# The way from attention to MLP in a fused kernel: weight memory laid out anew, rows of g spread by transfers, a rewritten tail

## The chip, the core and the metric

The kernel runs as one program on one core of a Trainium2 chip. The metric is the device time of an execution in microseconds (us). The engines are TensorE (PE, with its weight loads as PEld), VectorE (DVE), ScalarE (ACT), GpSimd (POOL) and SyncE (SP), whose queue issues the kernel's transfers. Each engine works through its instructions in the order of the program.

## The reference

Three blocks follow one another, all in float32:

```
attention (B 4, H 8, S 576, D 64; 2304 tokens of 512 after the heads are joined)
    q, k rotated by cos/sin;  attn = softmax(q k^T / 8);  x = attn v
soft MoE (8 experts, 4 slots each, so 32 slots; F 1024)
    logits = x @ phi                       # phi [512, 32]
    d = softmax over tokens (axis 0);  slot_input = d^T @ x
    slot_out[e] = relu(slot_input[e] @ w1[e]) @ w2[e]
    c = softmax over slots (axis 1);   x = c @ slot_out
MLP (512 -> 2048 -> 512)
    h = x @ w_in;  g = h * sigmoid(h);  out = g @ w_out
```

## The kernel before

**Attention.** Sixteen pairs of heads are worked through in one stream in which an order of PE is written out by hand, with tables of steps (W_LOADS, W_OUT_AT, BATCH) that say at which step of a pair a further task is put in. The MoE weights come as 64 loads of 512 KB, w_0 to w_63: w1 is w_0 to w_31, for layer 1, and w2 is w_32 to w_63, for layer 2. The first 23 (NWA) have memory of their own, the next four lie in two tiles of the rotary stage, and all further ones in the pool `wb`, which is opened after the attention in memory that the attention's pools leave. A load into such memory waits for the last instruction that used what lay there. SP issues all loads in the order of their numbers, and a load that waits keeps the next ones back; eight transfers at most are under way, since there are eight semaphores for them. Chunks of w_out whose numbers stand in W_OUT_EARLY are loaded and converted during the attention.

**The tail of the attention.** The soft MoE's sums over tokens are kept over half-batches. For the last one (`h1` in the code) PE makes logits `lgh1`, ACT and DVE the exponentials, PE the transposed weights `dps5`, DVE copies them to `dh1`, PE multiplies them with the tiles x12 to x15 (`sps5`), and `slots` merges the sum into `s_b0`, transposes it to `si` (the slot inputs) and works out the denominator `den`. `lt` gets the last transposed logits.

**The MoE layers.** Layer 1 (line 871) multiplies `si` with w1, in two halves of four experts; layer 2 (line 892) the hidden rows with w2, each expert in a column group of 32. Between the quarters of layer 2 other tasks are put: transposes of the combine weights `c` to `cs` (`t0`, `t1`, `t3`). `slot_t` copies layer 2's sum to `o`, transposes it, and copies it to `so`, the slot outputs.

**The MLP.** Since x = c @ slot_out, the kernel multiplies slot_out with w_in once, which gives 32 rows of g for each block of columns, spread over partitions and split in a high and a low part (`gs0`, `gs1`); `hps` = gs × cs is then the hidden layer. The first 128 columns come from `g0_ps`, the next 384 from `g_product(0)` and `g_all`, and three further blocks of 512 from `g_product(1)` to `(3)`, each followed by 16 copies that spread its rows (`g_copy`, line 1103 on ACT and 1105 on DVE). The main loop has 3 blocks of tokens × 16 chunks of 128 hidden columns. A step has one chunk's sigmoid, split and 6 × 3 products with w_out (`ops`, lines 1154 to 1156); G_STEPS says behind which product of the first steps a g product or its copies stand. A chunk of w_out is 512 KB of 64-bit words which `narrow` converts (ACT `hw`, two DVE operations), and `split_hl` splits into `wo_hi` and `wo_lo`. Chunks 0 and 1 are converted together as `wf_first`, ahead of the loop.

## Time and profile before

| | us |
|---|---|
| median of 3 runs | 571.57 (571.24 to 571.92) |
| the profiled execution's own time | 573.27 |
| its span on the core | 571.5 |
| PE busy | 540.4 |
| DVE busy | 316.9 |
| ACT busy | 307.9 |

The span is the time from the first to the last instruction of the profiled execution. Busy times overlap between engines; the granted clock of PE was 0.982 of full speed as a mean over the span. Of the stages, the attention ends at about 300.6 us, layer 1 at 317, layer 2 at 338, and the main loop starts at 346.

### The profile page before, as it was taken

How to read it: one execution, taken by the hardware profiler on the slowest of the kernel's cores; microseconds unless marked ns; L12 is line 12 of the kernel's file. 1: busy time of each engine (PE TensorE's matmuls, PEld its weight loads, DVE VectorE, ACT ScalarE, POOL GpSimd, SP SyncE). 2: the span in 40 equal slices, each digit the busy share in tenths (PEclk: the TensorE clock that was granted, in tenths of full speed). 3: DMA queues.
4: the chain of work that ended last, by engine and by line, in shares of the span. 5: the costliest groups of instructions: out<-in, count | busy, mean ns of one | idle time of the engine just before them, and what ended most of it. 6: DMA issues, size and time to landing. Idle time of an engine off the chain costs nothing.

```text
span 571.5 us, 15141 instructions
## 1 busy us (share of the span) xinstructions
PE 540.4 (95%) x6219; PEld 438.1 (77%) x6219; DVE 316.9 (55%) x841; ACT 307.9 (54%) x612; POOL 111.3 (19%) x96
## 2 busy tenths in 40 slices
PE   5599999999999999999979989899999999999997
PEld 2378989898897998888853337677888888888885
DVE  4756666766666567654130457697454444544442
ACT  2366667666767566664421327987554433544332
POOL 4933332313333323200000021133000000000000
PEclk9679999999999999999998999999999999999999
DMA  8226777635665575743799895422020000200003
GB/s 301 95 56 206 266 244 278 203 116 172 224 231 172 207 265 166 249 166 107 296 322 382 306 359 179 135 93 75 0 93 18 1 1 1 96 16 0 2 0 111
DMA packets 36773, 88.70 MB, mean 155 GB/s; under 512 B 10560, under 2 KB 11872, under 8 KB 34784
## 3 DMA queue, kind: packets, MB, share of 16 engines
q1 hardware_dynamic: 36694, 87.73, 44.3%
q8 instruction: 49, 0.80, 0.6%
q14 instruction: 20, 0.16, 0.1%
q10 hardware_dynamic: 10, 0.00, 0.0%
HBM read 78.20 MB, written 7.60 MB: 150 GB/s over the span
## 4 chain that ended last, share of the span: by engine, by line
PE 76%; ACT 10%; DVE 5%; DMA 4%; issue 3%; POOL 1%; SPq 1%; ACTq 0%; DVEq 0%
PE u L386 10%; PE ops L1156 10%; PE ops L1154 10%; PE ops L1155 10%; PE st L353 8%; PE psmx L300 3%; PE st_r L366 3%; PE l L871 3%; PE hps L1049 3%; ACT e L357 3%; PE xps L414 3%; DMA w_out_raw<-in_w_out_dram 2%; PE psmx L316 2%; ACT relu L308 2%; PE u L380 2%
## 5 line engine op out<-in xcount | busy, mean ns | idle before, releaser
L1056 DVE TENSOR_TENSOR hps<-hps,g 128x384 f32<-128x384 f32 x96 | 49.8, 561 | 84.6 <-ACT g L1053 84.3
L1053 ACT ACTIVATE g<-hps 128x384 f32<-128x384 f32 x96 | 42.3, 490 | 82.3 <-PE hps L1049 81.9
L1154 PE MATMUL ops<-wo_hi,ghi 128*128 128x512 f32 x216 | 84.7, 392 | 0.0
L1155 PE MATMUL ops<-wo_lo,ghi 128*128 128x512 f32 x216 | 84.4, 391 | 0.0
L1156 PE MATMUL ops<-wo_hi,glo 128*128 128x512 f32 x216 | 84.3, 390 | 0.0
L321 DVE CUSTOM_DVE_ANT_0 relu<-psmx,relu 128x288 f32<-128x288 f32 x140 | 57.7, 455 | 47.1 <-ACT e L357 36.3
L357 ACT ACTIVATE e<-st 128x512 f32<-128x512 f32 (+1 forms) x128 | 76.4, 650 | 10.9 <-PE st L353 10.9
L386 PE MATMUL u<-v,e 128*64 128x65 f32 x2048 | 80.6, 225 | 0.0
L386 PEld LDWEIGHTS u<-v,e 128*64 128x64 f32 x2048 | 71.5, 139 | 6.2 <-issue 3.0
L308 ACT ACTIVATE relu<-psmx 128x576 f32<-128x576 f32 x62 | 40.1, 652 | 51.7 <-PE psmx L300 33.6
L259 POOL TENSOR_TENSOR raw<-raw,tab 128x576 f32<-128x576 f32 x29 | 41.8, 1442 | 132.8 <-DMA raw<-in_qk_dram 96.7
L1062 DVE TENSOR_TENSOR glo<-hps,ghi 128x384 fp32r<-128x384 f32 x96 | 49.4, 552 | 5.0 <-ACT ghi L1059 1.8
L1059 ACT ACTIVATE ghi<-hps 128x384 fp32r<-128x384 f32 x96 | 45.6, 494 | 10.2 <-DVE hps L1056 10.1
L1156 PEld LDWEIGHTS ops<-wo_hi,glo 128*128 128x128 f32 x216 | 40.6, 188 | 8.5
L1155 PEld LDWEIGHTS ops<-wo_lo,ghi 128*128 128x128 f32 x216 | 40.6, 188 | 7.5 <-issue 0.4
L1154 PEld LDWEIGHTS ops<-wo_hi,ghi 128*128 128x128 f32 x216 | 40.6, 188 | 7.5 <-issue 0.2
L256 POOL TENSOR_TENSOR raw<-raw,tab 128x576 f32<-128x576 f32 x29 | 42.0, 1447 | 0.0
L353 PE MATMUL st<-hi 64*128 64x256 f32 (+1 forms) x256 | 39.7, 302 | 0.0
L353 PE MATMUL st<-mq,neg_a 64*128 64x256 f32 (+1 forms) x256 | 39.1, 297 | 0.6 <-DMA mq<-m 0.6
L353 PE MATMUL st<-hi,lo 64*128 64x256 f32 (+1 forms) x256 | 38.9, 296 | 0.0
L353 PE MATMUL st<-lo,hi 64*128 64x256 f32 (+1 forms) x256 | 38.9, 296 | 0.0
L397 DVE TENSOR_SCALAR r<-u 128x4 f32<-128x4 f32 (+1 forms) x32 | 5.2, 164 | 49.7 <-PE u L388 30.1
(223 smaller groups left out, 998.7 us busy)
## 6 DMA issues: line engine op xcount, KB each, us to landing
w<-in_w_dram SPq DMA_DIRECT2D x64, 512.0 KB
raw<-in_qk_dram SPq DMA_DIRECT2D x14, 1152.0 KB
w_out_raw<-in_w_out_dram SPq DMA_DIRECT2D x16, 512.0 KB
w_in_raw<-in_w_in_dram SPq DMA_DIRECT2D x12, 512.0 KB
v<-in_v_dram SPq DMA_DIRECT2D x16, 325.0 KB
out_dram<-os SPq DMA_DIRECT2D x18, 256.0 KB
raw<-in_qk_dram SPq DMA_DIRECT2D x4, 576.0 KB
w_in<-w_in SPq DMA_DIRECT2D x8, 256.0 KB
```

The source lines that it names most:

```text
L308: act.activation(out=r, in_=pair[:, :, 0:HS], func=ACTF.Relu)
L321: dve.tensor_tensor_reduce(out=r[:, hd], in0=t[hd], in1=r[:, hd], scale=1.0, scalar=-3.0e38, op0=ALU.add, op1=ALU.max, accum_out=mxs[p % 2 ...
L353: pe.matmul(st[:, hd, 0:n], lhsT=a, rhs=b, start=i == 0, stop=i == 3, skip_group_check=True)
L357: act.activation(out=e[:, :, 0:n], in_=st[:, :, 0:n], func=ACTF.Exp, scale=0.125)
L386: pe.matmul(u[q:q + 64, 2 * i + hd], lhsT=e[:, hd, o:o + 64], rhs=x[:, hd], start=n == 0 and i + hd == 0, stop=n == 4, skip_group_check=True)
L1053: act.activation(out=g[i], in_=t[i], func=ACTF.Sigmoid)
L1056: dve.tensor_tensor(out=t[i], in0=t[i], in1=g[i], op=ALU.mult)
L1059: act.activation(out=ghi[:, i], in_=t[i], func=ACTF.Copy)
L1062: dve.tensor_tensor(out=glo[:, i], in0=t[i], in1=ghi[:, i].bitcast(F32), op=ALU.subtract)
L1154: pe.matmul(t, lhsT=a, rhs=wo_hi[k], start=k == 0, stop=False)
L1155: pe.matmul(t, lhsT=a, rhs=wo_lo[k], start=False, stop=False)
L1156: pe.matmul(t, lhsT=b, rhs=wo_hi[k], start=False, stop=k == 15)
```

## The change

- FREED gives the 20 weights of the pool `wb` other places: the order of the loads stays, but the sixth and seventh (w_33, w_34) get the pool's positions 16 and 17, and later ones the positions that they had. The attention's own pools are laid out in another order beneath.
- The memory of the rotary table (`tab`) becomes a pool of its own that stays open: w_27 is loaded into it, and later the split chunk 11 of w_out lies there.
- The tail: `xps15_1` and the other transposes stand elsewhere, `slots` no longer scales and adds on DVE but multiplies `s_b0` with a scaled identity `ss` and adds the second sum in PSUM, `si` is one copy, `den` comes behind (`total`), and ACT copies `lt`.
- `slot_t` copies `o` in two halves, on ACT and DVE. Chunk 0 of w_out is loaded early in place of chunk 12, so that only chunk 1 is left in `wf_first`, and it is converted behind the first products. Products of the first two token groups stand ahead of `g_all`.
- `g_copy` becomes 16 transfers on SP for each g product, in place of 12 copies on ACT and 4 on DVE, right behind the product.
- In the attention another of the two tiles for `relu` is used at u = 4.

```diff
-W_LOADS = (14, 18, 24, 27, 34, 37, 45, 54, 64, 66, 76, 86, 96, 102, 108, 114, 127, 129, 125, 135, 133, 123, 137, 145, 148, 134, 139)
+W_LOADS = (14, 18, 24, 27, 34, 37, 45, 54, 64, 66, 76, 86, 96, 102, 108, 114, 127, 129, 125, 135, 133, 123, 137, 145, 148, 134, 139, 138)
 SCALES = -19
-W_OUT_EARLY = (3, 6, 9, 12)
+W_OUT_EARLY = (0, 3, 6, 10)
 W_OUT_AT = (23, 43, 83, 113)
 EARLY = -10
+WO_TAB = 11
+FREED = (0, 1, 2, 3, 4, 16, 17, 5, 6, 7, 8, 9, 10, 11, 12, 18, 19, 13, 14, 15)
 WO_SLOT = {12: 13, 13: 14, 14: 15, 15: 16}
 QO = (0, 256, 576)
 QN = (256, 320)
 
-G_STEPS = (5, 7, 16, 19, 28, 14, 23, 37, 46, 53, 58)
-ACT_QUADRANTS = (0, 1, 2)
+G_STEPS = (5, 22, 52)
+LOAD_STEP = 28
+CONV_STEPS = (14, 23, 37, 44)
...
+    p_tab = ctx.enter_context(tc.tile_pool(name="tab", bufs=1, side=left))
...
+        elif n == 4:
+            w_sb[i, h, e] = p_tab.tile([128, 2, S], F32, tag="tab", name=f"w_{m}").rearrange("p t s -> p (t s)")[:, 0:1024].rearrange("p (k f) -> p k f", k=k)
...
-            p_tab, p_k, p_relu, p_14, p_soft, p_q, p_15, p_e, p_v, p_s, p_r = (mkpool(n, 1) for n in ("tab", "k", "relu", "p14", "soft", "q", "p15", "e", "v", "s", "r"))
+            p_k, p_relu, p_14, p_q, p_15, p_e, p_v = (mkpool(n, 1) for n in ("k", "relu", "p14", "q", "p15", "e", "v"))
+            xqp = mkpool("xq", 6)
+            p_s, p_soft = mkpool("s", 1), mkpool("soft", 1)
             xp = mkpool("xp", 4)
-            xqp = mkpool("xq", 6)
+            p_r = mkpool("r", 1)
...
-                r = p_e.tile([128, 2, QN[1]], F32, tag=f"e{u}", name=f"relu{p}_{u}")[:, :, 0:HS] if p == 0 and u in (2, 3) else relus[u % 2]
+                r = p_e.tile([128, 2, QN[1]], F32, tag=f"e{u}", name=f"relu{p}_{u}")[:, :, 0:HS] if p == 0 and u in (2, 3) else relus[1 if u == 4 and p > 1 else u % 2]
...
-                        act.activation(out=s_b[0][64:128], in_=s_b[0][64:128], func=ACTF.Copy, scale=sc[64:128, 5:6])
+                        ps["ss"] = p_r.tile([128, 3, NSLOT], F32, tag="dh0", name="ss")[:, 0]
+                        dve.tensor_scalar(out=ps["ss"], in0=stack_i[:, 0:NSLOT], scalar1=sc[:, 5:6], scalar2=None, op0=ALU.mult)
...
-                def slots():
-                    acc = s_b[0]
-                    for j in range(2):
-                        w = slice(256 * j, 256 * j + 256)
-                        dve.scalar_tensor_tensor(out=acc[0:64, w], in0=acc[0:64, w], scalar=sc[0:64, 5:6], in1=ps["s"][0:64, w], op0=ALU.mult, op1=ALU.add)
-                    t2 = ps_mx.tile([128, 2, 512], F32, tag="mx", name="si_ps")
-                    for j in range(2):
-                        t = t2[:, j]
-                        for k in range(2):
-                            c0 = 256 * j + 128 * k
-                            pe.matmul(t[:, NSLOT * k:NSLOT * k + NSLOT], lhsT=acc[:, c0:c0 + 128], rhs=stack_i[:, 0:NSLOT], start=True, stop=True)
-                        dve.tensor_copy(out=si[:, 2 * j:2 * j + 2], in_=t[:, 0:64].rearrange("p (k s) -> p k s", k=2))
+                def slots(t):
+                    o = hb[1][0:64, 0:DM]
+                    act.activation(out=o[:, 0:256], in_=ps["s"][0:64, 0:256], func=ACTF.Copy)
+                    dve.tensor_copy(out=o[:, 256:512], in_=ps["s"][0:64, 256:512])
+                    for k in range(4):
+                        pe.matmul(t[:, NSLOT * k:NSLOT * k + NSLOT], lhsT=s_b[0][:, 128 * k:128 * k + 128], rhs=ps["ss"], start=k == 0, stop=False, skip_group_check=True)
+                    for k in range(4):
+                        pe.matmul(t[:, NSLOT * k:NSLOT * k + NSLOT], lhsT=o[:, 128 * k:128 * k + 128], rhs=stack_i[0:64, 0:NSLOT], start=False, stop=True, skip_group_check=True)
+                    dve.tensor_copy(out=si, in_=t[:, 0:4 * NSLOT].rearrange("p (k s) -> p k s", k=4))
+
+                def total():
                     dve.tensor_tensor(out=scs[:, 3:5], in0=sc[:, 3:5], in1=sb[:, 3:5], op=ALU.mult)
...
-            for i in range(NWA + 4):
+            for i in range(NWA + 5):
...
-            h1[0]((0, 1, 2))
+            h1[0]((0,))
+            x_15(1)
+            h1[0]((1, 2))
             assert not tasks, tasks
             h0[3]()
             h0[5]()
-            x_15(1)
             h1[0]((3,))
             h1[2]()
             h0[4]()
             h1[3]()
+            h0[6]()
+            h0[8]()
+            h1[5]()
             h1[4]()
-            h0[6]()
-            h1[5]()
-            h0[8]()
+            t = ps_mx.tile([128, 2, 512], F32, tag="mx", name="lt3_ps")
             h1[6]()
-            t = ps_st.tile([128, 2, 512], F32, tag="st", name="lt3_ps")[:, 0]
+            h1[7](t[:, 1])
             for i, (o, n) in enumerate(CHUNKS[3]):
-                pe.transpose(t[0:n, NSLOT * i:NSLOT * i + NSLOT], hb[2][0:32, o:o + n], ident[0:32, 0:32])
-            h1[7]()
-            dve.tensor_copy(out=lt[:, 15:19], in_=t[:, 0:4 * NSLOT].rearrange("p (c s) -> p c s", c=4))
-            dve.tensor_copy(out=lt[0:64, 19], in_=t[0:64, 4 * NSLOT:5 * NSLOT])
+                pe.transpose(t[0:n, 0, NSLOT * i:NSLOT * i + NSLOT], hb[2][0:32, o:o + n], ident[0:32, 0:32])
+            act.activation(out=lt[:, 15:19], in_=t[:, 0, 0:4 * NSLOT].rearrange("p (c s) -> p c s", c=4), func=ACTF.Copy)
+            act.activation(out=lt[0:64, 19], in_=t[0:64, 0, 4 * NSLOT:5 * NSLOT], func=ACTF.Copy)
+            h1[9]()
...
-        for i in range(NWA + 4, NW):
-            slot_w(i)
-        for i in range(NWA + 4, NW):
+        for i in range(NW - NWA - 5):
+            slot_w(NWA + 5 + FREED.index(i))
+        for i in range(NWA + 5, NW):
...
-            act.activation(out=o, in_=op[g], func=ACTF.Copy)
+            act.activation(out=o[:, 0:256], in_=op[g][:, 0:256], func=ACTF.Copy)
+            dve.tensor_copy(out=o[:, 256:512], in_=op[g][:, 256:512])
...
-        load_wo(0)
...
-            t, h = (wa.tile([128, 2, 512], F32, tag=f"w{i}", name=n) for i, n in ((3, "wf_first"), (4, "hw_first")))
-            for k in range(2):
-                first.append((t[:, k], narrow(raw_w.pop(k), t[:, k], None, None, hw=h[:, k])))
+            t, h = (wa.tile([128, 512], F32, tag=f"w{i}", name=n) for i, n in ((3, "wf_first"), (4, "hw_first")))
+            first.append((t, narrow(raw_w.pop(1), t, None, None, hw=h)))
 
         first = []
         layer2(1, (t0, t1, t3))
         slot_t(1)
 
-        for f in first[0][1]:
-            f()
...
+        elif k == WO_TAB:
+            t = p_tab.tile([128, 2, S], F32R, tag="tab", name=f"wo_hl{k}")
+            wo_hi[k], wo_lo[k] = t[:, 0, 0:DM], t[:, 1, 0:DM]
...
-    def g_copy(n, r):
-        for q in range(4):
-            c0 = 512 * (n % 2) + 128 * r
-            o, i = gs2[n // 2][32 * q:32 * q + 32, c0:c0 + 128], gfull[n][q // 2][32 * r:32 * r + 32].bitcast(F32)
-            if q in ACT_QUADRANTS:
-                act.activation(out=o, in_=i, func=ACTF.Copy)
-            else:
-                dve.tensor_copy(out=o, in_=i)
+    def g_copy(n):
+        for r in range(4):
+            for q in range(4):
+                c0 = 512 * (n % 2) + 128 * r
+                sp.dma_start(out=gs2[n // 2][32 * q:32 * q + 32, c0:c0 + 128].bitcast(F32), in_=gfull[n][q // 2][32 * r:32 * r + 32].bitcast(F32))
...
+    def products(j, k, i, ghi, glo):
+        if k == 0:
+            ops[j, i] = ps_o.tile([128, DM], F32, tag="o", name=f"ops{j}_{i}")
+        t = ops[j, i]
+        a, b = ghi[:, 128 * i:128 * i + 128], glo[:, 128 * i:128 * i + 128]
+        pe.matmul(t, lhsT=a, rhs=wo_hi[k], start=k == 0, stop=False)
+        pe.matmul(t, lhsT=a, rhs=wo_lo[k], start=False, stop=False)
+        pe.matmul(t, lhsT=b, rhs=wo_hi[k], start=False, stop=k == 15)
...
-        (wf0, _), (wf1, n1) = first
+        wf1, n1 = first[0]
+        split_hl(0, wf_early[0], dve)
...
-        hidden(*seq[0], between=lambda: (split_hl(0, wf0, dve), g_product(0)))
+        hidden(*seq[0], between=lambda: g_product(0))
         n1[0]()
+        for i in range(2):
+            products(0, 0, i, *gt[0, 0])
...
-    for x, f in zip(G_STEPS, (lambda: g_product(1), lambda: copies(1), lambda: g_product(2), lambda: copies(2), lambda: load_last(1),
-                              lambda: conv_last(0), lambda: conv_last(1), lambda: conv_last(2), lambda: conv_last(3), lambda: g_product(3), lambda: copies(3))):
-        extra.setdefault(divmod(x, 6), []).append(f)
-    ops = {}
+
+    def put(x, f):
+        extra.setdefault(divmod(x, NI), []).append(f)
+
+    for n in range(1, 4):
+        put(G_STEPS[n - 1], lambda n=n: g_product(n))
+        put(G_STEPS[n - 1], lambda n=n: g_copy(n))
+    put(LOAD_STEP, lambda: load_last(1))
+    for k, x in enumerate(CONV_STEPS):
+        put(x, lambda k=k: conv_last(k))
```

In SP's queue, the loads around the first one that waits for the attention's last matmuls stand so before (w_39 to w_46; the names of the semaphores that a load waits for are in brackets, DMAHW being the one of the transfer eight places ahead):

```order
L120 DMA w_39_4990<-in_w2_dram 128x2x512 [waits DMAHW5_49]
L120 DMA w_40_4991<-in_w2_dram 128x2x512 [waits DMAHW6_49]
L120 DMA w_41_4992<-in_w2_dram 128x2x512 [waits DMAHW7_49]
L120 DMA w_42_4993<-in_w2_dram 128x2x512 [waits DMAHW0_49]
L120 DMA w_43_4994<-in_w2_dram 128x2x512 [waits DMAHW1_49,DVE_49,PE_49]
L120 DMA w_44_4995<-in_w2_dram 128x2x512 [waits DMAHW2_49,Activation_49]
L120 DMA w_45_4996<-in_w2_dram 128x2x512 [waits DMAHW3_49]
L120 DMA w_46_4997<-in_w2_dram 128x2x512 [waits DMAHW4_49]
```

and so in the change (w_31 to w_38):

```order
L126 DMA w_31_4985<-in_w1_dram 128x1024 [waits DMAHW5_49]
L126 DMA w_32_4986<-in_w2_dram 128x2x512 [waits DMAHW6_49,PE_49]
L126 DMA w_33_4998<-in_w2_dram 128x2x512 [waits DMAHW7_49,DVE_49,PE_49]
L126 DMA w_34_4999<-in_w2_dram 128x2x512 [waits DMAHW0_49]
L126 DMA w_35_4987<-in_w2_dram 128x2x512 [waits DMAHW1_49]
L126 DMA w_36_4988<-in_w2_dram 128x2x512 [waits DMAHW2_49]
L126 DMA w_37_4989<-in_w2_dram 128x2x512 [waits DMAHW3_49]
L126 DMA w_38_4990<-in_w2_dram 128x2x512 [waits DMAHW4_49,Activation_49]
```

The wait for DVE and PE together stands at w_43 before, and at w_33 in the change; the numbers of the loads go on in order in both.

On PE, at the end of the attention, the rows from the last `sps5` matmuls to the first of layer 1 are these before (`lt3_ps` are the transposes for `lt`, `si_ps` those for `si`):

```order
L565 MATMUL sps5_4918<-x12_3946,dh1_4862 32x64 x2
L565 MATMUL sps5_4918<-x13_4242,dh1_4862 32x64 x2
L565 MATMUL sps5_4918<-x14_4541,dh1_4862 32x64 x2
L565 MATMUL sps5_4918<-x15_4751,dh1_4862 32x64 x2
L842 MATMUL lt3_ps_4935<-cst_sb_73,last_logits_4826 128x32 x4
L842 MATMUL lt3_ps_4935<-cst_sb_73,last_logits_4826 64x32
L580 MATMUL si_ps_4943<-cst_sb_73,s_b0_77 128x32 x4
L871 MATMUL l1_0_0_5037<-w_0_653,si_79 32x512
L871 MATMUL l1_0_0_5037<-w_1_777,si_79 32x512
```

and these in the change:

```order
L574 MATMUL sps5_4922<-x12_3946,dh1_4864 32x64 x2
L574 MATMUL sps5_4922<-x13_4242,dh1_4864 32x64 x2
L574 MATMUL sps5_4922<-x14_4543,dh1_4864 32x64 x2
L574 MATMUL sps5_4922<-x15_4753,dh1_4864 32x64 x2
L584 MATMUL lt3_ps_4921<-ss_4902,s_b0_80 128x32 x4
L586 MATMUL lt3_ps_4921<-cst_sb_76,last_logits_4828 128x32 x4
L852 MATMUL lt3_ps_4921<-cst_sb_76,last_logits_4828 128x32 x4
L852 MATMUL lt3_ps_4921<-cst_sb_76,last_logits_4828 64x32
L881 MATMUL l1_0_0_5039<-w_0_653,si_82 32x512
L881 MATMUL l1_0_0_5039<-w_1_777,si_82 32x512
```

The transposes for `si` are now twice four, the second from a copy of the sum, and stand ahead of those for `lt`.

In the main loop, the copies that spread the rows of `g_product(1)` stand on ACT before, between the split of step 2 and the sigmoid of step 3:

```order
L1059 ACTIVATE ghi0_2_5491<-hps0_2_1_5500 128x384
L1095 ACTIVATE gh1_5536<-g_ps1_5519 128x128
L1103 ACTIVATE gs0_5343<-gh1_5536 32x128 x2
L1103 ACTIVATE gs0_5343<-gl1_5537 32x128
L1103 ACTIVATE gs0_5343<-gh1_5536 32x128 x2
L1103 ACTIVATE gs0_5343<-gl1_5537 32x128
L1103 ACTIVATE gs0_5343<-gh1_5536 32x128 x2
L1103 ACTIVATE gs0_5343<-gl1_5537 32x128
L1103 ACTIVATE gs0_5343<-gh1_5536 32x128 x2
L1103 ACTIVATE gs0_5343<-gl1_5537 32x128
L1053 ACTIVATE g0_3_0_5573<-hps0_3_0_5571 128x384
L1053 ACTIVATE g0_3_1_5580<-hps0_3_1_5578 128x384
```

In the change ACT has no such rows, and SP's queue has the transfers there, `x2` for two of them:

```order
L130 DMA w_out_raw5_5488<-in_w_out_dram 128x1024
L130 DMA w_out_raw9_5742<-in_w_out_dram 128x1024
L1112 DMA gs0_5342<-gh1_5535 32x128 x2
L1112 DMA gs0_5342<-gl1_5536 32x128 x2
L1112 DMA gs0_5342<-gh1_5535 32x128 x2
L1112 DMA gs0_5342<-gl1_5536 32x128 x2
L1112 DMA gs0_5342<-gh1_5535 32x128 x2
L1112 DMA gs0_5342<-gl1_5536 32x128 x2
L1112 DMA gs0_5342<-gh1_5535 32x128 x2
L1112 DMA gs0_5342<-gl1_5536 32x128 x2
L130 DMA w_out_raw7_5616<-in_w_out_dram 128x1024
L130 DMA w_out_raw8_5661<-in_w_out_dram 128x1024
```

The loads of w_out chunks 7 and 8 stand behind the sixteen transfers.

## Rows read from the trace of the kernel before

**Rows 1.** The page: busy time, share of the span and instructions of PE.

```profile
PE 540.4 (95%) x6219; PEld 438.1 (77%) x6219; DVE 316.9 (55%) x841; ACT 307.9 (54%) x612; POOL 111.3 (19%) x96
```

**Rows 2.** Busy time of each engine by stage, granted clock, DMA share, GB/s.

```profile
283.00:300.60 17.60, 13.55 (x235) 9.86 (x232) 6.14 (x24) 4.92 (x14) 0.00 (x0) 1.00 0.90 316
300.60:317.20 16.60, 16.60 (x136) 5.98 (x137) 2.93 (x5) 2.73 (x5) 2.23 (x2) 0.90 0.91 335
317.20:338.10 20.90, 20.47 (x166) 7.97 (x161) 8.90 (x24) 5.07 (x12) 0.00 (x0) 1.00 0.99 372
338.10:346.05 7.95, 5.07 (x83) 3.75 (x83) 4.63 (x8) 5.55 (x13) 4.37 (x3) 1.00 0.43 174
346.05:375.00 28.95, 27.11 (x173) 20.83 (x172) 22.34 (x50) 24.48 (x62) 3.86 (x3) 1.00 0.48 164
```

**Rows 3.** PE's waits from 283 to 375: in total, times, longest.

```profile
PE hps L1049 <- DVE glo L1062: 1.8, 3, 1.2
PE l L871 <- DVE lt L845: 1.6, 1, 1.6
PE hps L1049 <- DVE gs L929: 1.0, 1, 1.0
...
PE g_all L1110 <- ACT gf L1092: 0.7, 1, 0.7
...
PE lgh L514 <- ACT xt L418: 0.5, 1, 0.5
```

**Rows 4.** Waits of SP's own queue from 255 to 350, columns as in rows 3.

```profile
SPq L120 <- PE l L871: 14.4, 4, 7.6
...
SPq L120 <- PE st L353: 10.5, 2, 10.2
```

**Rows 5.** Busy time by stage, columns as in rows 2, around a stop of SP.

```profile
268.00:280.00 12.00, 11.42 (x229) 10.26 (x227) 2.91 (x8) 5.76 (x10) 0.00 (x0) 1.00 0.91 345
280.00:286.00 6.00, 5.69 (x124) 5.08 (x120) 0.76 (x3) 2.53 (x5) 0.00 (x0) 1.00 0.45 155
286.00:298.80 12.80, 10.64 (x171) 7.28 (x167) 4.88 (x16) 3.80 (x11) 0.00 (x0) 1.00 0.90 318
```

**Rows 6.** SP in order of time from 296.84: start, length, issue.

```profile
296.85 2.71 SPq L120 DMA_DIRECT2D w<-in_w_dram  x5
```

**Rows 7.** The chain that ended last, 283 to 302: start, length, what.

```profile
296.24 0.59 PE sps L565 x16
...
300.18 0.19 DVE lt L844
...
300.60 1.92 PE l L871 x9
```

**Rows 8.** Transfers from 319 to 331: GB/s in forty slices.

```profile
GB/s 171 177 328 403 355 314 389 410 362 389 417 382 369 375 348 335 410 382 376 389 403 382 375 410 389 396 416 410 389 389 416 403 389 382 403 375 396 307 355 396
```

**Rows 9.** Busy time by stretch, columns as in rows 2, where the clock is asked.

```profile
298.20:301.44 3.24, 1.47 (x12) 0.86 (x16) 1.40 (x9) 0.00 (x0) 0.00 (x0) 1.00 0.99 339
301.44:304.85 3.41, 3.41 (x20) 1.08 (x16) 0.00 (x0) 0.00 (x0) 0.00 (x0) 0.50 1.05 399
342.00:346.00 4.00, 2.22 (x41) 1.79 (x42) 2.88 (x6) 2.48 (x7) 1.79 (x2) 1.00 0.03 12
```

**Rows 10.** Transfers from 346 to 354: GB/s in forty slices.

```profile
GB/s 0 0 0 0 0 0 20 143 225 143 184 143 369 164 246 307 410 451 369 430 410 430 410 410 430 451 369 348 328 287 205 82 41 41 20 20 41 20 0 0
```

**Rows 11.** SP in order of time from 346 to 350, columns as in rows 6.

```profile
346.37 0.38 SPq L176 DMA_DIRECT2D w_in_raw<-in_w_in_dram  x1
```

**Rows 12.** Transfers from 296 to 332: GB/s in forty slices.

```profile
GB/s 300 68 148 330 407 376 380 401 412 398 382 362 346 376 357 346 405 387 376 412 328 87 30 150 375 130 330 353 391 387 353 391 391 396 401 396 394 380 362 380
```

**Rows 13.** PE in order of time before 338.2, columns as in rows 6.

```profile
336.17 1.94 PE L892 MATMUL l<-w,ht 128*32 128x512 f32 x16
```

**Rows 14.** Line 1103: ns min/median/max, first and last start.

```profile
L1103 ACT ACTIVATE gs<-gh x24: 307/309/311, 355.3 to 401.1; 32x128 fp32r<-32x128 f32 x24
```

**Rows 15.** Tile bd, its small transfers, columns as in rows 14.

```profile
L279 SPq DMA_DIRECT2D bd<-lo x32: 493/592/1435, 15.5 to 254.8; - x32
```

More of the change, by code (lines that the diff above doesn't have):

```diff
@@ L586, in slots @@
                     dve.reciprocal(out=den, in_=den)
-                return logits, logits2, soft, expo, keep, d_t, s_mm, slots, merge
+                return logits, logits2, soft, expo, keep, d_t, s_mm, slots, merge, total
             CHUNKS = [[(128 * c, min(128, S - 128 * c)) for c in range(5)]] * 4
@@ L1113, in attn_softmoe_mlp_kernel @@
     seq = [(j, k) for j in range(NBLK) for k in range(16)]
+    ops = {}
+    def products(j, k, i, ghi, glo):
[6 more added lines that the diff above has]
+        pe.matmul(t, lhsT=b, rhs=wo_hi[k], start=False, stop=k == 15)
     def dummy(n):
@@ L1136, in attn_softmoe_mlp_kernel @@
     hidden(*seq[1])
-    def copies(n):
-        for r in range(4):
-            g_copy(n, r)
     extra = {}
-    for x, f in zip(G_STEPS, (lambda: g_product(1), lambda: copies(1), lambda: g_product(2), lambda: copies(2), lambda: load_last(1),
-                              lambda: conv_last(0), lambda: conv_last(1), lambda: conv_last(2), lambda: conv_last(3), lambda: g_product(3), lambda: copies(3))):
-        extra.setdefault(divmod(x, 6), []).append(f)
-    ops = {}
+    def put(x, f):
[6 more added lines that the diff above has]
+        put(x, lambda k=k: conv_last(k))
     for n, (j, k) in enumerate(seq):
@@ L1149, in attn_softmoe_mlp_kernel @@
         for i in range(NI):
-            if k == 0:
-                ops[j, i] = ps_o.tile([128, DM], F32, tag="o", name=f"ops{j}_{i}")
+            if (j, k, i) not in ((0, 0, 0), (0, 0, 1)):
+                products(j, k, i, ghi, glo)
             t = ops[j, i]
-            a, b = ghi[:, 128 * i:128 * i + 128], glo[:, 128 * i:128 * i + 128]
-            pe.matmul(t, lhsT=a, rhs=wo_hi[k], start=k == 0, stop=False)
-            pe.matmul(t, lhsT=a, rhs=wo_lo[k], start=False, stop=False)
-            pe.matmul(t, lhsT=b, rhs=wo_hi[k], start=False, stop=k == 15)
             if (n, i) in extra:
```

## The prediction

> **What bounds the kernel now.** I read the page first, then the table of stages, the waits of PE, the waits and transfers of SP, and the chain. The page says that PE is busy for 540.4 of 571.5 us [rows 1]: PE is the bound, and a change can win only PE's idle time, or lose by making more of it. The stages show where it lies [rows 2]: 17.60 − 13.55 = 4.05 us in the last 17.6 us of the attention, none in layer 1, 20.90 − 20.47 = 0.43 in layer 2, 7.95 − 5.07 = 2.88 in the head of the MLP, 1.84 in the first 29 us of the main loop. The waits name the pieces [rows 3]: `lt` 1.6, `gs` 1.0, `g_all` 0.7, and in the loop `hps` on `glo` 1.8. The change touches all four. The question is what it does to the transfers of the MoE weights. In layer 2 they are hidden now, at a DMA share of 0.99 and 372 GB/s [rows 2], so with little room.
>
> **The weights, the largest term.** SP issues its transfers strictly in the order written; one that waits holds up all behind it. That shows now: SP stood for up to 10.2 us at a weight load that waited for PE's `st` [rows 4], and the DMA share was 0.45 from 280 to 286 us, beside 0.91 before and 0.90 after [rows 5]. The next such stop ended at 296.85, when five loads (w_43 to w_47) went out in a row [rows 6]; the first of them waits for PE, and the chain has the last matmuls of `sps5` end at 296.24 + 0.59 = 296.83 [rows 7]. From w_43 to w_63, 21 loads start there or later.
>
> After the change FREED gives w_33 position 16 of the pool `wb`. In the built program this is bytes 187,776 to 191,872 of a partition, on which the tiles x14 (187,136 to 189,440) and x13 (189,440 to 191,744) lay before. The last instructions that read x14 are matmuls of `sps5`, and in SP's order w_33 waits for DVE and PE. So the stop sits at w_33 in place of w_43: **31 loads instead of 21 start after it**, with only w_28 to w_32 ahead.
>
> When does w_63 arrive? Undisturbed, most slices move 375 to 416 GB/s and the 12 us as a whole 372, with the first slices still filling [rows 8]. A load of 524,288 bytes takes 1.35 us at 389, 1.41 at 372, and 1.31 at the 399 of another stretch [rows 9]; I take 1.35, as 389 is the commonest value of the full slices. The stop: `sps5` moves forward by something between nothing and the 0.5 us for which the logits wait for `xt` [rows 3], since the transposes `xps15_1` that `xt` comes from now stand further ahead on PE, while the copy of `dh1` goes behind the merge on DVE. I take 0.2, so the stop ends at 296.6, bounds 296.3 and 296.9. A transfer into an empty queue, issued at 346.37, shows its first bytes about 1 us later, and a group thins out for 1 to 2 us at its end [rows 10, 11]; I take 1.0 and 2.0. Then 296.6 + 1.0 + 31 × 1.35 + 2.0 = **341.4**. The other way round: ten loads more are 13.5 us, less the hole of some 3 us that the flow has now at 315 to 319 [rows 12], where SP waits for `l` of layer 1 [rows 4] and where the later queue will be full; that makes w_63 10.5 us later.
>
> Layer 2 ends with w_63's own work. Sixteen matmul instructions, four column groups beside each other with four in a row, take 1.94 us [rows 13]; w_63 alone has four in a row in one group, about 1.9 us. So 341.4 + 1.9 = 343.3 in place of 338.1 [rows 2]: **+5.2 us**, bounds +4.0 (1.31 a load) and +7.1 (1.41). Layer 1 uses w_0 to w_31, all there early, and may start 1.8 us sooner: 296.83 to 300.60 is now the way from `sps5` to it [rows 7], with two `si` copies and five small DVE operations; after the change one `si` copy is left on that way, and the `den` operations come behind. This only lengthens layer 2's wait. Layer 2 takes 20.90 us for 32 weights, 0.65 each [rows 2]; started at 315.4, its second half begins at 325.9, w_48 arrives at 296.6 + 1.0 + 16 × 1.35 + 2.0 = 321.2, and with 0.65 against 1.35 us PE has caught up at the seventh of its sixteen weights. The last eight come one by one.
>
> The Trainium skill (DMA: Bandwidth & Descriptors, Specifications) puts a core's share of HBM at about 358 GB/s. By that a load takes an estimated 1.46 us, and the sum would come out 3.4 us higher, near 578.3; the stretch at 399 GB/s is above it, and the measurement decides.
>
> **The head of the MLP.** `gs` came 1.0 us late [rows 3] while DVE still converted `wf_first`; that conversion is now for one chunk and behind the first products. `g_all` waited 0.7 for `gf` [rows 3]; six products now fill that time. Against this, the split copy of `o` is serial (its second half, on DVE, waits for the first, on ACT, since both write one tile), and `wo_lo0` stands ahead of the copy of `so` on DVE: 0.4 to 0.8 more, by the usual 0.3 to 0.7 of such copies. −1.0 − 0.7 + 0.8 = **−0.9**, bounds −1.3 and 0. The load of w_in_n0 is right behind w_63 on SP and lands 2 us after it, ahead of its first use; this costs nothing, but another 2 us there would show.
>
> **The g rows in the loop.** 36 copies of 0.31 us leave ACT [rows 14], 12 leave DVE. Neither is the bound, so the gain is the idle time of PE behind them: of its 1.8 us on `glo`, 1.2 is one piece [rows 3], at the end of the first twelve copies; the loop's first 29 us hold 1.84 in all [rows 2]. SP issues 48 transfers of 32×128 in their place. The nearest row is 0.59 us for the issue of a small one [rows 15], so 9.5 us for 16, and the order puts w_out_raw7 and 8 behind the first group and w_in_raw3_1 behind the second. A new wait of 0 to 3 us in the loop is possible; I take 0.8, as the first user stands several steps later. −1.8 + 0.8 = **−1.0**, bounds −1.8 and +1.2.
>
> The attention costs nothing: the order of PE, DVE and ACT is the same up to its tail, and the other maximum tile for u = 4 is one that PE does not wait for; bounds ±0.5.
>
> **Sum.** +5.2 − 0.9 − 1.0 = +3.3. The profiled execution had a span of 571.5 and took 573.27, the median of the runs shown is 571.57: the span goes to 574.8, and the median to **574.9**, 0.6% slower. About 0.2% (1.1 us) is what a measurement here can tell from no change.
>
> **The rivals.**
> - *w_33 does not hold layer 2 up*: its stop ends long before `sps5`, or the flow makes it up. Then count the tail's 1.8, the head and the loop: 571.57 − 1.8 − 0.9 − 1.0 = 567.9, and 566.4 if the half clock behind the tail goes too (3.41 us at a granted 0.50, the 1.2 GHz level, after a stretch with PE busy for 1.47 of 3.24 us [rows 9]: some 1.5 us). For it: the slack of the loads can't be read from PE, which waits for none now. Against it: at the best rate seen (1.31) w_63 is still at 340.2. It decides if w_63 arrives before 341.4 − 3.3 = 338.1: a stop that ends at 293.3, or 1.24 us a load (423 GB/s). Chance 0.16.
> - *Forecast*: PE waits for the last weights, 574.9. Chance 0.58.
> - *The clock falls while PE waits for weights*, as it did after the stretch above. w_63's 1.9 us grow by 1.6 and the head's 5.07 us of work by as much: 574.9 + 3.2 = 578.1. Against it: 1.9 us of work for a weight that comes each 1.35 leave PE with something at all times, and from 342 to 346, busy for 2.22 of 4.00, it kept its clock [rows 9]. Chance 0.12.
> - *The small transfers hold up the loop*: a step's `hps`, or the conversions of chunks 7 and 8, wait for SP; loop +1.2 for −1.0, 577.1. Chance 0.09.
> - The rest, 0.05, are sums near zero: the late arrival with a larger gain behind it.
>
> Faster by over 0.2%: 0.17, the first rival and a little of the rest. Within 0.2%: 0.08, the rest and the forecast's lower end. Slower: 0.75. The range leaves the first rival out and takes in the bounds of loads, head and loop and the clock: 571.9 to 578.4.
>
> **What will show it.** Right: w_33 issued between 296 and 297, a DMA share near 0 from about 282 to there, PE waiting for DMA of `w` in layer 2's second half, which ends near 343; `gs` no longer behind `wf_first`; SP's small issues and no ACT copies to `gs` in the loop. Wrong: w_33 issued before 293, no wait of PE for `w`, or over 4 us of idle PE in the loop.

## The result, and the profile after

The changed kernel takes 579.88 us (median of 4 runs, 578.56 to 580.74), the kernel before 571.75 in the same comparison: 1.2% slower, ratio 1.012 with a 95% interval of 1.0096 to 1.0143. The forecast was 574.9 with a range to 578.4. The direction and its main cause were right; the loss is 8.1 us and not 3.3.

The page of the changed kernel, its PE row (busy time, share, instructions), the clock granted to PE in forty slices, and GB/s in the same slices:

```profile
PE 547.6 (95%) x6227; PEld 440.1 (76%) x6227; DVE 316.6 (55%) x828; ACT 296.8 (51%) x578; POOL 111.5 (19%) x96
...
PEclk9589999999999999999999999999999999999999
...
GB/s 300 128 47 233 244 226 262 202 188 165 234 219 110 201 264 237 226 167 199 43 175 390 387 401 231 96 103 173 16 69 42 1 0 1 91 20 0 1 0 111
```

PE is busy for 7.2 us more than in [rows 1] with almost the same work. The slice with 43 GB/s (274 to 288 us) is where the loads stood still. The waits of SP's own queue (in total, times, longest) and SP's issues in order of time say why:

```profile
SPq L126 <- PE sps L574: 19.8, 1, 19.8
SPq L126 <- DMA w<-in_w_dram: 15.3, 22, 0.9
```

```profile
294.54 5.48 SPq L126 DMA_DIRECT2D w<-in_w_dram  x10
```

w_33 waited 19.8 us for `sps5` and went out at 294.54. (Everything up to the tail lies about 2 us earlier in this execution than in that of [rows 7], from its first microseconds on, so 294.5 here is 296.6 there. This also is why the two spans, 576.8 and 571.5, differ by less than the medians.) By stage, columns as in [rows 2]:

```profile
280.00:286.00 6.00, 5.69 (x133) 4.71 (x131) 0.00 (x0) 2.40 (x5) 0.00 (x0) 1.00 0.00 0
286.00:298.00 12.00, 10.17 (x131) 6.90 (x135) 5.40 (x21) 3.21 (x12) 0.00 (x0) 1.00 0.20 61
...
316.00:327.00 11.00, 11.00 (x74) 3.71 (x66) 1.93 (x8) 0.38 (x1) 0.00 (x0) 1.00 1.05 387
327.00:344.00 17.00, 15.63 (x69) 5.78 (x69) 5.61 (x16) 2.90 (x8) 0.28 (x1) 1.00 1.04 394
```

No byte moves from 280 to 286, and later the flow is full at 387 to 394 GB/s. That PE looks busy from 327 to 344 is a trap: the table of waits names no wait for `w` either. PE in order of time (start, length) shows it:

```profile
327.34 4.06 PE L902 MATMUL l<-w,ht 128*32 128x512 f32 x16
...
332.11 4.66 PE L902 MATMUL l<-w,ht 128*32 128x512 f32 x16
...
338.75 3.43 PE L902 MATMUL l<-w,ht 128*32 128x512 f32 x16
```

The sixteen instructions that took 1.94 us in [rows 13] now take 3.4 to 4.7, because the column groups no longer run beside each other: each starts as its weight comes, and one is always at work. The last group ends at 338.75 + 3.43 = 342.18.

In the main loop, PE's waits from 283 to 410, for [rows 3]:

```profile
PE hps L1059 <- DVE glo L1072: 2.4, 3, 1.1
PE hps L1059 <- DVE gl L1106: 1.3, 1, 1.3
PE ops L1129 <- ACT ghi L1069: 1.3, 2, 0.8
...
PE g_ps L1145 <- DVE so L919: 0.5, 1, 0.5
PE otp L916 <- ACT o L912: 0.5, 1, 0.5
```

`lt`, `gs` and `g_all` are gone, as forecast; `ghi` is new, and the waits for DVE in the loop have grown (`glo` and `gl` took 1.8 and 0.5 us in the kernel before over the same work). SP's issues there:

```profile
369.38 1.22 SPq L1112 DMA_DIRECT2D gs<-gl  x2
370.70 1.00 SPq L130 DMA_DIRECT2D w_out_raw<-in_w_out_dram  x2
374.03 1.15 SPq L1112 DMA_DIRECT2D gs<-gh  x2
...
383.17 1.22 SPq L1112 DMA_DIRECT2D gs<-gl  x2
384.49 0.53 SPq L182 DMA_DIRECT2D w_in_raw<-in_w_in_dram  x1
```

A group of sixteen occupies SP for 10.4 us (374.03 to 384.39), and the chain that ended last runs through both groups and then through the load behind them:

```profile
383.80 0.59 SPq L1112
...
384.49 5.34 DMA w_in_raw<-in_w_in_dram
389.84 0.67 ACT hw L140
390.54 0.44 DVE w_in L143
```

**All kernels by stage.** Each number is a difference of two times read from that kernel's timeline: the end of `sps5`, the first matmul of layer 1, the last end of layer 2, the end of the span. The last column is the mean time of those runs in which the granted clock was at least 0.983 as a mean over the run, and their number. It is needed since the times hang on the clock: over the 77 runs of the kernel before that stand beside the experiments, 9 with 0.983 or more took 570.96 as a mean, 26 with 0.980 to 0.982 took 572.84, and 42 with 0.979 or less 574.42. The ratios below are over all runs.

| kernel | `sps5` to layer 1 | layers 1 and 2 | end of layer 2 to end | time at clock 0.983+ |
|---|---|---|---|---|
| before | 3.80 | 37.50 | 233.37 | 570.96 (9) |
| changed | 2.79 | 44.78 | 234.65 | 579.76 (4) |
| e1, w_33 elsewhere | 2.79 | 35.87 | 235.51 | 571.16 (9) |
| e2, copies | 2.79 | 45.80 | 233.35 | 578.82 (5) |
| e3, both | 2.79 | 35.86 | 233.43 | 569.24 (5) |
| e4, before, w_33 and w_43 swapped | 3.79 | 44.30 | 236.19 | none |
| e5, e1 and the load ahead | 2.79 | 35.87 | 237.64 | none |
| e7, e3 and one copy of o | 2.79 | 35.86 | 238.18 | 572.34 (4) |
| e8, before with the tail | 2.79 | 39.19 | 234.05 | 572.35 (8) |
| e9, e3 and products back | 2.79 | 35.86 | 233.49 | 569.75 (7) |
| e10, e3 and idle transfers | 4.68 | 37.39 | 238.99 | 574.67 (8) |
| e12, e1 with w_38 in that place | 2.79 | 38.18 | 234.45 | 573.77 (11) |
| e13, e1 with half the transfers | 2.79 | 35.86 | 231.08 | 566.71 (4) |

At a clock of 0.983 and above the change costs 8.8 us. The profiled executions show what the mean clock counts: those at 0.983 or more have no stretch at a granted 0.50 between 40 us and the last 3 us, those at 0.980 to 0.982 have one of 3.41 us, that of e4, at 0.979, two, and that of e10, at 0.976, three on end. One costs 1.7 us: layer 1 took 16.80 us with it in the kernel before and 15.10 without it in the changed one. In the table such stretches lie in the second column of before, e4 and e8, in the first two of e10, and in the third of e4, e5 and e7. Each row is one execution; e2 has the loads and the layers of the changed kernel and took 1.0 us longer for them, so the second column holds to about 1 us.

### The profile page after: what moved, and what is told of

It is laid out like the page before. It is cut to its first block, busy times and chain, and to the rows that moved or that the text cites. A ratio compares the mean times of both kernels' runs of the same rounds, so it can differ in the third digit from the quotient of the medians.

```text
span 576.8 us, 15165 instructions
## 1 busy us (share of the span) xinstructions
PE 547.6 (95%) x6227; PEld 440.1 (76%) x6227; DVE 316.6 (55%) x828; ACT 296.8 (51%) x578; POOL 111.5 (19%) x96
## 4 chain that ended last, share of the span: by engine, by line
PE 69%; DMA 11%; ACT 7%; DVE 4%; issue 4%; SPq 3%; POOL 1%; ACTq 0%; DVEq 0%
PE u L394 10%; PE ops L1129 10%; PE ops L1131 10%; PE ops L1130 9%; PE st L361 8%; DMA w<-in_w_dram 7%; PE psmx L308 3%; PE st_r L374 3%; SPq L1112 3%; ACT e L365 3%; PE xps L422 3%; PE hps L1059 2%; PE psmx L324 2%; ACT relu L316 2%; PE u L388 2%
## 5 line engine op out<-in xcount | busy, mean ns | idle before, releaser
L1129 PE MATMUL ops<-wo_hi,ghi 128*128 128x512 f32 x198 | 77.4, 393 | 1.3 <-ACT ghi L1069 1.3
L1131 PE MATMUL ops<-wo_hi,glo 128*128 128x512 f32 x198 | 77.4, 392 | 0.0
L1130 PE MATMUL ops<-wo_lo,ghi 128*128 128x512 f32 x198 | 76.9, 390 | 0.0
L267 POOL TENSOR_TENSOR raw<-raw,tab 128x576 f32<-128x576 f32 x29 | 42.4, 1463 | 129.6 <-DMA raw<-in_qk_dram 104.0
L1131 PEld LDWEIGHTS ops<-wo_hi,glo 128*128 128x128 f32 x198 | 37.2, 188 | 8.4 <-DVE glo L1072 0.3
L1129 PEld LDWEIGHTS ops<-wo_hi,ghi 128*128 128x128 f32 x198 | 37.1, 188 | 8.2 <-ACT ghi L1069 1.9
L264 POOL TENSOR_TENSOR raw<-raw,tab 128x576 f32<-128x576 f32 x29 | 42.7, 1472 | 0.0
L1130 PEld LDWEIGHTS ops<-wo_lo,ghi 128*128 128x128 f32 x198 | 37.2, 188 | 6.8 <-issue 0.2
L1129 PE MATMUL ops<-wo_hl,ghi 128*128 128x512 f32 x90 | 35.2, 391 | 0.0
```

The source lines that it names most:

```text
L264: eng.tensor_tensor(out=r[:, i, 0, w], in0=r[:, i, 0, w], in1=tab[:, 0, w], op=ALU.mult)
L1129: pe.matmul(t, lhsT=a, rhs=wo_hi[k], start=k == 0, stop=False)
L1130: pe.matmul(t, lhsT=a, rhs=wo_lo[k], start=False, stop=False)
L1131: pe.matmul(t, lhsT=b, rhs=wo_hi[k], start=False, stop=k == 15)
```

## The experiments

**e1, the place of one weight.**

```diff
-FREED = (0, 1, 2, 3, 4, 16, 17, 5, 6, 7, 8, 9, 10, 11, 12, 18, 19, 13, 14, 15)
+FREED = (0, 1, 2, 3, 4, 17, 5, 6, 7, 8, 9, 10, 11, 12, 18, 19, 13, 14, 16, 15)
```

The weights in between move up by one position each.

> The changed kernel with one edit: pool position 16, which lies on x14 and x13, goes to w_46 in place of w_33, and w_33 gets position 17. If the wait of w_33 for sps5 is what layer 2 loses by, SP's long stop (19.8 us in the changed kernel) sits at w_44 with 20 loads behind it in place of 31, w_63 lands some 11 us sooner, PE has no wait for weights in layer 2, and the time falls by 6 to 8 us, to 572 to 574. If the loads had been hidden all the same and the loss is in the main loop or the clock, the time falls by less than 2 us.

571.27 us, 8.6 below the changed kernel; ratio to before 0.9978 (0.9948 to 1.0008), in place of 1.012. Layers 1 and 2 take 8.9 us less, SP's wait for `sps5` is 4.0 us and holds 20 loads, and the last sixteen matmul instructions run beside each other again (SP's waits, then PE in order of time):

```profile
SPq L126 <- PE sps L574: 4.0, 1, 4.0
```

```profile
331.68 1.94 PE L902 MATMUL l<-w,ht 128*32 128x512 f32 x16
```

The place of this one weight is what the change lost by.

**e2 and e3, the rows of g by copies again.**

```diff
-                sp.dma_start(out=gs2[n // 2][32 * q:32 * q + 32, c0:c0 + 128].bitcast(F32), in_=gfull[n][q // 2][32 * r:32 * r + 32].bitcast(F32))
+                o, i = gs2[n // 2][32 * q:32 * q + 32, c0:c0 + 128], gfull[n][q // 2][32 * r:32 * r + 32].bitcast(F32)
+                if q < 3:
+                    act.activation(out=o, in_=i, func=ACTF.Copy)
+                else:
+                    dve.tensor_copy(out=o, in_=i)
```

with the products, copies and conversions at the steps of the kernel before. e3 has the edit of e1 too.

> The changed kernel with the rows of g spread by copies on ACT (12 of 16) and DVE (4) again, at the steps of the kernel before, and everything else as changed. If the 32 transfers that stand one behind the other on SP delay w_out_raw7, w_in_raw3_1 and gs, the idle time of PE in the loop falls from 4.2 us to about 2.5 and the time by 1.5 to 3 us, to 577 to 578.4. If the loop's loss comes from the products moved ahead of g_all or from the late start, the time is the same within 0.5 us or higher.

> Both edits of the two kernels run beside it: the place of w_33 and the copies on ACT and DVE. If the two causes add, the time is 570 to 571, some 9 us under the changed kernel and 1 to 2 us under the kernel before, from the shorter tail and the shorter head. If the tail's gain of 3 us is only moved into a later wait, it is 572 or above.

e2: 578.97, ratio 1.009 (1.0062 to 1.0117); e3: 569.35, ratio 0.9924 (0.9898 to 0.9951). From layer 2's end to the end, the transfers (with the steps that go with them) cost 234.65 − 233.35 = 1.3 us in the changed kernel, and 235.51 − 233.43 = 2.1 where the weights come in time. Of these, 0.4 and 0.7 us stand behind the last matmul: from its end to the end of the span it takes 4.24 us in the changed kernel and 4.55 in e1, 3.81 in e3 and 3.82 in the kernel before. All five kernels with 48 transfers take 4.13 or more there; why is open. The two causes add up to within 1 us (8.6 and 0.9 alone, 10.5 together), and without them the kernel is faster than before: by 0.76%, but the kernel before had the lower clock in most of its runs there. At 0.983 and above it is 1.7 us over all runs of the kernel before and 1.0 against the two of that comparison; by stages, it is the 1.0 us of the tail.

**e4, the wait alone, in the kernel before.**

```diff
-            slot_w(i)
+            slot_w({33: 43, 43: 33}.get(i, i))
```

> The kernel before with one edit: w_33 and w_43 change places in the pool, so that the load that waits for sps5 is the sixth and not the sixteenth of those after the attention. If that wait costs what the changed kernel lost, 10 loads more come after it, layer 2 ends 5 to 6 us later, and the time is 576.5 to 578. If the transfers have room to catch up, the time stays within 1 us of 571.7.

580.41, ratio 1.0109 (1.0085 to 1.0132), so 6.3 us over the 574.13 of before in that comparison. SP's stop is 23.5 us, and layers 1 and 2 take 44.30. One swap of two places does to the old kernel what the whole change did.

```profile
SPq L120 <- DVE dh L554: 23.5, 1, 23.5
```

**e12, a place in between.**

```diff
+FREED = (0, 1, 2, 3, 4, 17, 5, 6, 7, 8, 16, 9, 10, 11, 12, 18, 19, 13, 14, 15)
```

> The changed kernel with pool position 16 given to w_38, so that 26 loads in place of 31 stand behind the wait for sps5. By the sum that fits the changed kernel (first load complete 3.1 us after its issue, 1.36 us for each further one, 1.9 for the last one's matmuls) layer 2 ends 1.8 us later than with the place that waits for nothing, layers 1 and 2 take 37.7 us together in place of 35.9 and 44.8, and the time is 1.2 to 2.4 us above that of the kernel with w_33 moved. If the wait costs as a whole or not at all, it is one of these two.

573.83, ratio 1.0009 (0.9989 to 1.0029). Layers 1 and 2 take 38.18, 2.3 more than in e1 where 1.8 was expected, and at the same clock the time is 573.77 against 571.16, 2.6 more. SP's stop:

```profile
SPq L126 <- PE sps L574: 8.7, 1, 8.7
```

With 20, 26 and 31 loads behind the stop, the layers take 35.87, 38.18 and 44.78: with 20 nothing is lost (the last sixteen instructions take 1.94 us in e1 and 3.38 here), and from 26 to 31 it is 1.3 us for each further load.

**e10, the transfers alone.** 48 transfers are added to e3, into a tile that nobody reads; the copies stay.

```diff
+    scr = g2.tile([128, 512], F32, tag="scr", bufs=1, name="scr")
+    def idle_sends(n):
+        for r in range(4):
+            for q in range(4):
+                sp.dma_start(out=scr[32 * q:32 * q + 32, 128 * r:128 * r + 128], in_=gfull[n][q // 2][32 * r:32 * r + 32].bitcast(F32))
```

> The kernel with both edits (w_33 moved, rows of g spread by copies on ACT and DVE), with 48 further transfers on SP, 16 behind each g product, that write the same rows into a tile that nobody reads. If SP's time for a group (10 us) is what costs the loop, by holding up the loads behind it, the loop is 1.5 to 2.5 us longer than without them, and from layer 2's end to the end it takes 235 to 236 us in place of 233.4. If what costs is that the consumers of g wait for the transfers, or the other steps of the products, it stays at 233.2 to 233.9.

574.74, ratio 1.0047 (1.0018 to 1.0077); 233.43 becomes 238.99. So 48 transfers whose result nobody waits for cost 5.6 us (5.4 at a clock of 0.983 or more), over twice what was expected. They hold up the loads behind them, and PE waits longer for what DVE makes of these (in e3 the two waits take 2.6 and 0.4 us in all):

```profile
378.88 1.22 SPq L1124 DMA_DIRECT2D scr<-gl  x2
380.15 0.58 SPq L131 DMA_DIRECT2D w_out_raw<-in_w_out_dram  x1
380.82 0.39 SPq L183 DMA_DIRECT2D w_in_raw<-in_w_in_dram  x1
```

```profile
PE hps L1060 <- DVE glo L1073: 3.2, 4, 1.4
PE g_ps L1100 <- DVE glo L1073: 1.4, 1, 1.4
```

In e3 this load of w_in_raw went out at 362.69, with layer 2's end 6.1 us earlier there. Against e1, with as many transfers and no copies, the copies on ACT and DVE, with their other steps, cost 238.99 − 235.51 = 3.5 us. (Its profiled execution had the clock fall in the tail, which the first two columns show and the third does not contain.) The same transfers in another engine's queue were not tried.

**e5, one load ahead of the transfers.** e1, with

```diff
         put(G_STEPS[n - 1], lambda n=n: g_product(n))
+        if n == 2:
+            put(G_STEPS[n - 1], lambda: load_last(1))
         put(G_STEPS[n - 1], lambda n=n: g_copy(n))
-    put(LOAD_STEP, lambda: load_last(1))
```

> The changed kernel with w_33 moved as in the first experiment, and one more edit: the load of w_in_raw3_1 is issued right behind the second g product and ahead of its sixteen transfers, in place of behind them. If the 10 us that SP needs for a group of sixteen is what makes this load late (it landed at 381.1 us and DVE's conversions and hps came late after it, with three waits of PE of 0.95, 1.14 and 0.90 us), these three shrink to under 1.2 us together, and from the end of layer 2 to the end of the kernel it takes 233.5 to 234.2 us in place of 235.5. If the transfers themselves or the moved steps are the cause, it stays at 235 to 236.

573.04, ratio 1.0002 (0.9978 to 1.0025): no better than e1. The late waits shrank to 1.00 and 0.67, but two new ones of 0.63 and 1.24 came near 375, and there the clock fell:

```profile
374.80:378.20 3.40, 1.53 (x5) 1.03 (x5) 3.37 (x7) 1.43 (x3) 1.39 (x1) 0.87 0.20 43
378.20:381.60 3.40, 3.40 (x11) 2.67 (x10) 2.02 (x5) 1.17 (x3) 0.00 (x0) 0.62 0.97 367
```

So it isn't this one load: less the 1.7 us of this stretch, the 237.64 us from layer 2's end are 235.9, no better than the 235.51 of e1. The w_out loads behind the second group went out at 376.6 us, as in e1.

**e13, half of the transfers.** e1, where q 0 and 1 (the high parts) go by transfers, q 2 by ACT and q 3 by DVE.

```diff
+                if q < 2:
+                    sp.dma_start(out=o.bitcast(F32), in_=i)
+                elif q == 2:
+                    act.activation(out=o, in_=i, func=ACTF.Copy)
+                else:
+                    dve.tensor_copy(out=o, in_=i)
```

> The changed kernel with w_33 moved, and half of the rows of g spread by transfers (8 of 16, those of the high part), the other half by copies on ACT (4) and DVE (4), at the change's steps. If the cost goes with the length of SP's groups, 5 us in place of 10, it takes 234.2 to 234.8 us from layer 2's end to the end, between 233.4 without transfers and 235.5 with all. If the steps at which g is made are the cause, it stays at 235.3 or above.

> The kernel with half of the transfers once more, since its profiled execution ran at a mean granted clock of 0.747 and says nothing of the loop. If SP's shorter groups are what made it the fastest so far, its first group of eight ends 5 us after its start, w_out_raw7 and w_in_raw3_1 are issued 5 us sooner than with sixteen, PE's idle time in the loop is under 3.4 us, and from layer 2's end to the end it takes 231 to 233 us. If it was the chip or the clock of those runs, it takes 234 to 235.5 us as expected before, and the ratio to before is 0.992 or above.

First run (e11): 566.69, ratio 0.9875 (0.9841 to 0.9909). Second (e13): 566.52, ratio 0.9893 (0.9853 to 0.9933). It is the fastest of all, 6.9 and 5.9 us below before, and 4.3 among the runs at the higher clock. (The profiled execution of the first ran at a mean granted clock of 0.747 and took 664.58, so it isn't in the ratio, and the second one's is shown.) 231.08 us from layer 2's end to the end is 4.4 below e1 and 2.4 below e3; the expectation of 234.2 to 234.8 had each half only save its share. SP's groups are 5 us long, and PE's waits for DVE in the loop fall to 1.1 us, from 4.2 in e1; those on `ghi` stay. And 0.7 of the 4.4 is the way behind the last matmul, 3.83 here. Against e3 the steps of the g products and copies differ too, and ACT makes 4 copies of 16 and not 12, so the 2.4 is not shown to come from the transfers alone.

```profile
352.16 5.03 SPq L1114 DMA_DIRECT2D gs<-gh  x8
...
365.10 4.96 SPq L1114 DMA_DIRECT2D gs<-gh  x8
370.16 0.53 SPq L182 DMA_DIRECT2D w_in_raw<-in_w_in_dram  x1
```

```profile
PE ops L1135 <- ACT ghi L1069: 1.3, 2, 0.8
PE hps L1059 <- DVE glo L1072: 1.1, 2, 0.7
```

**e8, the tail alone, in the kernel before** (the diff's hunks for `ss`, `slots`, `total` and the order of `h0`, `h1`).

> The kernel before with the change's tail alone: the new order of logits and transposes, the scaled identity, one si copy, den behind, lt on ACT. If the tail is what made the kernel with both edits faster than before, the way from sps5 to layer 1 falls from 3.8 to 2.8 us, PE's clock does not fall to 0.50 in layer 1, which takes 15.1 us in place of 16.8, and the time falls by 2 to 3.5 us. If the gain sits in the head and the loop, or a later load takes it back, the time stays within 1 us of before.

572.92, ratio 0.9991 (0.9973 to 1.001): no gain. The tail is 1.0 us shorter, but the clock fell all the same, with PE busy for 3.02 of the 3.40 us ahead:

```profile
295.60:299.00 3.40, 3.02 (x35) 2.48 (x33) 1.47 (x7) 0.73 (x3) 0.00 (x0) 1.00 0.40 128
299.00:302.40 3.40, 3.40 (x24) 0.85 (x20) 0.00 (x0) 0.00 (x0) 0.00 (x0) 0.50 1.00 361
```

and layer 2 took 1.7 us more than before. So it was in the profiled execution, at 0.982. Eight of the twelve runs had 0.983 or more, and they too gained nothing: 572.35, against 571.50 for the four such runs of the kernel before in that comparison. In the profiled execution's layer 2, the instructions from 320.75 on end with four of one column group alone, 0.43 us apart, where four groups ran beside each other before; their weights had been issued over 15 us earlier, and why PE took them in that order stays open, and so does whether the runs at the higher clock lost their microsecond there too.

**e7 and e9, two parts of the head**, each undone in e3:

```diff
-            act.activation(out=o[:, 0:256], in_=op[g][:, 0:256], func=ACTF.Copy)
-            dve.tensor_copy(out=o[:, 256:512], in_=op[g][:, 256:512])
+            act.activation(out=o, in_=op[g], func=ACTF.Copy)
```

```diff
-        for i in range(2):
-            products(0, 0, i, *gt[0, 0])
```

> The kernel with both edits (w_33 moved, copies on ACT and DVE), and o copied in one piece on ACT, not in two halves on ACT and DVE. If the two halves run one behind the other, the split brings nothing: the way from layer 2's end to so stays at 1.8 to 1.9 us or shrinks by up to 0.2, and the time stays within 0.5 us. If the split saved time, the way grows by 0.2 to 0.4.

> The kernel with both edits, and the six products back behind g_all as in the kernel before. If these products filled PE's wait for gf, a wait of g_all on gf of about 0.7 us comes back, and from the end of layer 2 to the end it takes 234.0 to 234.2 us in place of 233.4. If the wait was only exchanged for that of the first products on ghi (0.76 us), it stays at 233.2 to 233.6.

e7: 574.09, ratio 1.0009 (0.9988 to 1.0031). From layer 2's end to `g0_ps` it is 2.15 us for 1.94 in e3, so the split saves 0.2. The rest of its loss is in the loop, where one wait of `ops` on `ghi` took 1.80 and the granted clock was 0.75 behind it (a stretch at 0.50, 1.7 us); a shift of 0.2 us brought this about, by what way is open. e9: 569.26, ratio 0.9934 (0.991 to 0.9958), 233.49 us for 233.43. `g_all` waits 0.46 for `gf`, and the 0.75 of the first product on `ghi` is gone: one wait was exchanged for the other.

## Why the prediction was wrong, step by step

- **Where it went.** Of the 4.3 us between the forecast's +3.3 and the +7.6 of the stages (last item), 1.1 are the weights, 0.9 the head, which brought nothing by the end, and 2.3 the loop. The range was also narrower than its own bounds: loads +7.1, head 0 and loop +1.2 make 579.9 and not 578.4.
- **w_33 holds the loads up: right in mechanism, 1 us too small.** The stop sat where it was said and ended when it was said (296.6 by the old execution's clock). From the end of `sps5` to the end of layer 2 it took 294.61 to 342.18, 47.6 us, for a forecast of 343.3 − 296.6 = 46.7. The rate was as taken (387 to 394 GB/s are 1.33 to 1.35 us a load). The term that was too small is start and end of the flow: w_63's first matmul ran at 340.28, 45.7 us after the issue of w_33, less 31 × 1.35 leaves 3.9, where 1.0 + 2.0 were taken. In e2 the same reckoning leaves 4.9, so this term varies by about 1 us from execution to execution. w_63's four matmuls alone took the forecast 1.9 us. The sign that was named, PE waiting for the DMA of `w`, did not show: matmuls that trickle count as busy, so "no wait of PE for w" was no sign of being wrong. The rule of the Trainium skill (DMA: Bandwidth & Descriptors, Specifications), 358 GB/s, would have put the total nearer to the result, 578.3, but for the wrong reason. The flow was 8 to 10% faster than that rule.
- **The head: −0.9 forecast, 0.3 at most measured.** The 37th product of `ops` starts 18.39 us behind layer 2's end, 18.71 before, with one `hps` matmul less ahead of it. In e3, which has no transfers, even this is gone at the end: 233.43 us, the kernel before 233.37. The waits for `gs` and `gf` did go (1.0 and 0.7), as said. The step that failed is the one that let them go without a successor: the first products wait 0.76 for `ghi` and those of the next step 0.50, which no term held. The halves of `o` do run one behind the other, but save 0.2 against one copy, and the way from layer 2's end to `g0_ps`, which the sum charged with 0.4 to 0.8, grew from 1.75 us to 1.85 (1.94 in e3).
- **The loop: −1.0 forecast, +1.3 measured, and this is the step that was wrong in kind.** The sum looked at when the rows land and found the first user several steps later. What costs is the transfers themselves: e10 shows 5.6 us for transfers that nobody waits for. During them SP issues nothing else for 10 us, twice within 24. The chain has 0.59 us of SP for each transfer and some 0.04 between two, so a group lasts as long as SP needs to issue it and does not wait for a free one of the eight places; the shorter groups of e13 fit this. Of the 1.3 us, 0.4 come behind the last matmul and not in the loop. That the copies on ACT and DVE are worth 3.5 us, more than PE's idle time behind them in [rows 3], was missed too. The prediction named w_out_raw7 and 8 and w_in_raw3_1 behind the groups, and its rival with a chance of 0.09 put the loop at +1.2.
- **The clock** did not fall while PE waited for weights (1.00 throughout), so that rival fell. In the changed kernel it stayed at 1.00 behind the tail as well, so layer 1 took 15.1 us and not 16.8; in that kernel this only lengthened the wait for the weights.
- The terms as measured, by stages: −1.0 (tail) + 7.3 (layers) + 1.3 (all after them) = +7.6, against +8.1 by the medians. Tail and layers together, +6.3, stand against the forecast's +5.2. The way from `sps5` to layer 1 got 1.0 us shorter and not 1.8, which the wait for the weights hides. The layers of the kernel before hold one stretch at 0.50; against e1, which has none, w_33 costs them 8.9.

## What to carry to other kernels

A load that is issued in order takes the latest release of all that stand ahead of it, so memory that comes free last belongs to the load that is issued last; one entry of a table cost 8.6 us here, and the kernel's own program shows such a wait before it runs. Many small transfers took the issuing queue's time, and here whoever stood behind them paid, not their reader: half of them, with the rest on the engines, was 4.4 us better than all and 2.4 better than none, where other steps had a part. A queue that has been just long enough to be hidden has no slack to read off PE's idle time, and matmuls that start one by one as their weights come look busy; compare their length with that of the same group elsewhere.

## What was not expected of the hardware

The times of one and the same kernel move with the granted clock of the run: 570.96 at 0.983 and above, 574.42 at 0.979 and below. Such a fall to 0.50 (1.2 GHz) came behind the tail with PE busy for 1.47 of 3.24 us before it [rows 9], and in e8 with 3.02 of 3.40; in the changed kernel PE was busy for 3.02 of 3.40 at the same place and it did not come. So neither a short tail nor PE's busy time there settles it. The changed kernel by stretch, for the rows of e8:

```profile
294.00:297.40 3.40, 3.02 (x40) 2.73 (x38) 1.09 (x5) 0.38 (x1) 0.00 (x0) 1.00 0.48 140
297.40:300.80 3.40, 3.40 (x34) 1.06 (x36) 0.38 (x3) 0.35 (x2) 0.00 (x0) 1.00 1.01 365
```
